# A piece of a weight matrix loaded as two transfers of 64 rows, in an attention and feed-forward kernel with a written-out order

## Chip, cores and metric

The kernel runs on one core of a Trainium2 chip. The core has a matrix engine (TensorE, in the profile PE, with its weight loads as PEld), a vector engine (VectorE, DVE), an engine for activation functions (ScalarE, ACT), a general one (GpSimd, POOL) and a queue engine that here only issues transfers (SyncE, SP). The transfers themselves run on 16 DMA engines, which the profile shows as one share. The metric is the time of the core on the device, in microseconds (us).

## What is computed

Two stages: an attention with 8 batches, 8 heads, 576 positions and 64 values a head, and a feed-forward layer on its 4608 tokens of 512 values.

```python
# attention: a pooled one (every 4 positions averaged) plus a local one (|i - j| < 4)
out_d = sm_attn(q_d, k_d, v_d)                  # softmax attention on 144 pooled positions
out_up = np.repeat(out_d, 4, axis=2)
scores = np.where(mask, scale * q @ k.T, -1e9)  # mask: |i - j| < 4
attn = softmax(scores)
x = (out_up + attn @ v)  -> [4608, 512]
# feed-forward
h = x @ w_in                                    # [512, 1024], in float64 as w_out and g_ln
solu = h * softmax(h)
ln = (solu - mean) / sqrt(var + 1e-6) * g_ln
return (ln @ w_out).astype(np.float32)
```

The weights come as 64-bit floats, the rest as 32-bit floats.

## The kernel before

Per batch, q and k are loaded and transposed, so that the 64 values of a head lie along the partitions; for the first two batches on PE against an identity (`EarlyBatch.pair_steps`, tiles qp and kp, L495), later on DVE. Sums over 4 positions (L380) give the pooled q and k (tiles qd_all and kd). The pooled attention (`Pooled`, tiles sd, pd, po) and the local one in windows of 64 positions (`Local`, L538 to L594, and `PairOfLocals`, tiles sc, pl, plt, xp) add up in a tile x for each batch; v is loaded in three forms (tiles vs, vt and vw).

The feed-forward layer works on 36 tiles of 128 tokens. `xhl` splits x into a high part xh and a low part xl. `ffn_in` multiplies: h takes 24 matmuls a tile (L778), three products (xh with wi_h, xh with wi_l, xl with wi_h) for 4 blocks of rows of w_in and 2 halves of its columns. After softmax and normalizing, the tile goes to DRAM and back in another order (L826, L858), is transposed on DVE (L879), split into uh (ACT, L885) and ul (POOL or DVE, L888), and `ffn_out` multiplies by wo_h and wo_l (L902).

The weights are converted first, in 16 pieces: pieces 0 to 7 are w_in, 8 to 15 w_out. A piece of w_in is 128 rows of 512 columns in 64 bits, 4 KB a row. A step `Weights.load` issues its transfer (L324). Then seven steps convert it (`piece` and `f32`): ACT takes the absolute value of the upper word (L333), DVE makes a 32-bit float in four instructions (L335, L339, L344, L348, tile w), ACT rounds it into wi_h (L371; for w_out with the gain ahead of it, L370), and POOL or DVE takes the rest into wi_l (L373). All eight pieces of w_in are needed for the first tile's h, since each piece gives columns of both halves. The raw words lie in a tile stage (pieces 0, 1, 6 and 7, two at a time) or w64 (the others; the profile calls both loads w and stage).

The rows of w_in are taken in the order in which the attention lays its heads: rows d of head r and of head r + 4 stand below each other. So a piece of w_in is two groups of 64 rows of the matrix, far from each other in DRAM, and its source has the shape 2 x 64 x 1024 words:

```python
by_pair = w_in.rearrange("(a r d) c two -> r a d c two", a=2, d=D)
self.src = [
    by_pair[cc, :, :, n * 512:(n + 1) * 512, :] for cc in range(NCC) for n in range(2)
] + [w_out[fc * P:(fc + 1) * P, :, :] for fc in range(NFC)]
```

The order of all work is written out. The function builds a list `plan` of 1871 steps (each a few instructions on one engine, or a transfer), and a table of numbers, `ORDER`, says in which order they are emitted; every engine then carries out its own instructions in that order. 24 of the steps (`keep_clock`, tile warm) are matmuls on zeros that only keep PE running. A second table, `OTHER`, lists the steps that go to the other of two engines (`engine`): for most DVE in place of POOL or ACT. All transfers are issued on SP, one after another.

Of the kernel before, what the change touches and what calls it, by code (L numbers as in the profile page):

```python
# [125 lines left out]
def pooled_local_attention_then_solu_ffn(  # L126
# [10 lines left out]
    nc = tc.nc  # L137
# [7 lines left out]
    NCC = DM // P  # L145
# [27 lines left out]
    def rows(n):  # L173
        return slice(n * 64, n * 64 + 64)
# [891 lines left out]
```

## Time and profile before

| | |
|---|---|
| three runs, us | 651.26 (median), 649.11 to 652.41 |
| the profiled execution, us | 651.89 |
| its span, first to last instruction, us | 650.1 |
| mean granted clock of PE | 0.952 |
| busy, us: PE, DVE, ACT, POOL | 559.6, 461.2, 309.8, 293.7 |
| DMA: moved, time of the packets as a share of 16 engines | 98.61 MB, 58.7% |

How to read the rows in the parts below: a row of the timeline has its start, its length, engine, line, operation, what is written and from what, and how often; behind it, in brackets, how long the engine had been idle and what ended that. A row of a table of stretches has its bounds, its length, and the busy time of PE, PEld, DVE, ACT and POOL in it, with the number of instructions, then the granted clock of PE (1 is full), the mean busy share of the 16 DMA engines and what they moved in GB/s. A row of waits has who waited, for whom, us in total, how often, and the longest. SPq is the time that SP takes to issue a transfer. A row of DMA issues has the size of one transfer and the median time from issue to landing.

### The profile page before, as it was taken

The numbers are of one execution on the slowest core, as the hardware profiler recorded it, in microseconds if no ns is written. First come the engines' busy times: TensorE is split into PE (matmuls) and PEld (weight loads), VectorE is DVE, ScalarE is ACT, GpSimd is POOL, SyncE is SP. The second block draws the span as 40 slices with busy tenths as digits, with TensorE's granted clock in tenths as the row PEclk, the third lists the DMA queues.
The fourth block names the chain that finished last, engine by engine and source line by source line (L and its number), as shares of the span: only waits on it lengthen the run. The fifth ranks groups of instructions, "written<-read, shape, count | busy, mean of one in ns | idle before, by whom it ended". The sixth has DMA issues, their size and how long they took to land.

```text
span 650.1 us, 16688 instructions
## 1 busy us (share of the span) xinstructions
PE 559.6 (86%) x6728; PEld 435.3 (67%) x6728; DVE 461.2 (71%) x724; ACT 309.8 (48%) x645; POOL 293.7 (45%) x443
## 2 busy tenths in 40 slices
PE   3135434998999999799998999999999999999997
PEld 1134233775677677577776777777777778778885
DVE  2333644897989888688976897899878787756442
ACT  1122324676585556336355365555454636354443
POOL 2002424388776764264654845344535325531211
PEclk9996757698999999999998999999999999999999
DMA  2333344978799688668874867795745345422420
GB/s 73 112 97 97 113 114 123 214 159 207 194 194 215 157 219 189 168 137 232 192 187 146 171 191 187 177 198 134 197 139 170 109 149 160 139 98 98 147 99 32
DMA packets 205854, 99.68 MB, mean 153 GB/s; under 512 B 161872, under 2 KB 192080, under 8 KB 205776
## 3 DMA queue, kind: packets, MB, share of 16 engines
q1 hardware_dynamic: 205776, 98.61, 58.7%
q8 instruction: 53, 0.87, 0.6%
q14 instruction: 25, 0.20, 0.1%
HBM read 65.54 MB, written 27.79 MB: 144 GB/s over the span
## 4 chain that ended last, share of the span: by engine, by line
PE 48%; DMA 18%; SPq 15%; DVE 10%; issue 3%; ACT 3%; POOL 2%; DVEq 0%; POOLq 0%; ACTq 0%
PE h L778 20%; PE o L902 20%; DMA w<-in_moe_w_in_dram 3%; SPq L480 3%; SPq L267 3%; DMA v<-u 3%; DMA stage<-in_moe_w_in_dram 2%; SPq L665 2%; DMA vs<-in_v_dram 2%; DMA u<-e 2%; DMA km<-in_k_dram 2%; SPq L858 2%; SPq L324 2%; PE po L754 2%; PE xp L589 1%
## 5 line engine op out<-in xcount | busy, mean ns | idle before, releaser
L778 PE MATMUL h<-wi_h,xh 128*128 128x512 f32 x288 | 118.1, 410 | 5.0 <-DVE e L793 5.0
L902 PE MATMUL o<-wo_h,uh 128*128 128x512 f32 x288 | 117.1, 407 | 3.6 <-ACT osb L909 2.8
L778 PE MATMUL h<-wi_h,xl 128*128 128x512 f32 x288 | 114.4, 397 | 0.0
L778 PE MATMUL h<-wi_l,xh 128*128 128x512 f32 x288 | 114.4, 397 | 0.0
L902 PE MATMUL o<-wo_l,uh 128*128 128x512 f32 x288 | 114.1, 396 | 0.0
L902 PE MATMUL o<-wo_h,ul 128*128 128x512 f32 x288 | 79.7, 399 | 0.0
L778 PEld LDWEIGHTS h<-wi_h,xh 128*128 128x128 f32 x288 | 54.6, 190 | 20.3 <-issue 5.9
L902 PEld LDWEIGHTS o<-wo_h,uh 128*128 128x128 f32 x288 | 54.0, 188 | 18.8 <-ACT osb L909 3.3
L888 POOL TENSOR_TENSOR ul<-v,uh 128x512 fp32r<-128x512 f32 x37 | 49.1, 1332 | 37.3 <-ACT uh L885 18.7
L902 PEld LDWEIGHTS o<-wo_h,ul 128*128 128x128 f32 x288 | 54.7, 190 | 13.3
L778 PEld LDWEIGHTS h<-wi_h,xl 128*128 128x128 f32 x288 | 54.4, 189 | 13.2
L778 PEld LDWEIGHTS h<-wi_l,xh 128*128 128x128 f32 x288 | 54.7, 190 | 11.9
L885 ACT ACTIVATE uh<-v 128x512 fp32r<-128x512 f32 x70 | 42.9, 624 | 40.7 <-DVE v L879 17.0
L902 PEld LDWEIGHTS o<-wo_l,uh 128*128 128x128 f32 x288 | 54.3, 189 | 11.7
L790 ACT ACTIVATE e<-h,nmx 128x1024 f32<-128x1024 f32 x36 | 40.0, 1112 | 44.4 <-DVE nmx L786 44.1
L495 PE MATMUL qp<-ident,qm 96*64 96x96 f32 x192 | 14.7, 328 | 50.7 <-DMA qm<-in_q_dram 50.5
L786 DVE TENSOR_REDUCE nmx<-h 128x1 f32<-128x1024 f32 x36 | 43.7, 1213 | 19.5 <-PE h L778 19.4
L879 DVE STREAM_TRANSPOSE v<-v 128x512 f32<-128x512 f32 x70 | 46.3, 688 | 13.8 <-DMA v<-u 13.8
L793 DVE SCALAR_TENSOR_TENSOR e<-h,e 128x1024 f32<-128x1024 f32 x36 | 43.6, 1212 | 17.4 <-ACT e L790 17.3
L798 POOL TENSOR_SCALAR nmu<-su 128x1 f32<-128x1 f32 x36 | 8.5, 236 | 94.6 <-DVE e L793 87.3
L335 DVE TENSOR_SCALAR w<-w 128x512 f32<-128x512 f32 x15 | 6.5, 440 | 62.6 <-ACT w L333 62.6
L495 PEld LDWEIGHTS qp<-ident,qm 96*64 96x64 f32 x192 | 13.0, 197 | 53.4 <-DMA qm<-in_q_dram 35.7
(124 smaller groups left out, 1113.0 us busy)
## 6 DMA issues: line engine op xcount, KB each, us to landing
u<-e SPq DMA_DIRECT2D x35, 512.0 KB, 3.0
v<-u SPq DMA_DIRECT2D x140, 128.0 KB, 2.9
qm<-in_q_dram SPq DMA_DIRECT2D x32, 288.0 KB, 12.4
km<-in_k_dram SPq DMA_DIRECT2D x32, 288.0 KB, 4.9
out_dram<-osb SPq DMA_DIRECT2D x36, 256.0 KB, 3.0
vs<-in_v_dram SPq DMA_DIRECT2D x64, 128.0 KB, 3.5
vw<-in_v_dram SPq DMA_DIRECT2D x80, 64.0 KB, 2.7
vw<-in_v_dram SPq DMA_DIRECT2D x40, 128.0 KB, 4.1
```

The source lines that it names most:

```text
L267: nc.sync.dma_start(vw[rows(par ^ wi), wi, :, :], v[b, 4 * par:4 * par + 4, s0:s0 + W, :].rearrange("h s d -> s h d"),)
L324: nc.sync.dma_start(hl, self.src[n])
L480: nc.sync.dma_start(t, src[self.b, pr::4].rearrange("h (p t) d -> p h (t d)", t=self.TT))
L495: nc.tensor.matmul(tp[rows(par), t // HT, at:at + self.TP], self.qk[nm, pr][:, par, t], ident[0:self.TP, 0:self.TP], start=True, stop=True,)
L778: nc.tensor.matmul(hps[:, n, :], src[:, cc, :], wt[:, cc, n * 512:(n + 1) * 512], start=(cc == 0 and src is xh and wt is wi_h), stop=(cc = ...
L786: nc.vector.tensor_reduce(out=nmx, in_=hf, op=ALU.max, axis=AX.X, negate=True)
L790: nc.scalar.activation(e, hf, AF.Exp, bias=nmx, scale=1.0, accum_out=se)
L793: nc.vector.scalar_tensor_tensor(out=e, in0=hf, scalar=1.0, in1=e, op0=ALU.mult, op1=ALU.mult, accum_out=su)
L879: nc.vector.transpose(vg, vg)
L885: nc.scalar.activation(uh, tp, AF.Copy)
L888: (usual if v is None else engine(usual, nc.vector)).tensor_tensor(out=ul, in0=tp, in1=uh.bitcast(F32), op=ALU.subtract)
L902: nc.tensor.matmul(o, src[:, j, :], wt[:, 4 * g + j, :], start=(g == 0 and j == 0 and src is uh and wt is wo_h), stop=(g == 1 and j == 3 a ...
```

## The change

`Weights.load` issues a piece of w_in as two transfers, one for each group of 64 rows; w_out is loaded as before. `ORDER` has the same 1871 steps in another order, and `OTHER` has 76 steps in place of 87.

```diff
 ORDER = """
-14 1 10 141 142 143 144 145 22 146 147 148 24 25 26 27 28 29 30 31 149 150 151 152 153 157 32 33
...
+25 24 141 2 142 143 144 11 14 26 145 146 27 28 147 32 148 149 157 29 30 31 150 151 152 153 33
...
 OTHER = """
-27 66 172 239 339 364 486 586 603 697 726 736 776 801 813 873 888 891 893 895 900 909 934 959
...
+172 239 536 543 553 580 637 659 661 699 719 751 776 811 863 865 881 883 940 965 972 984 1009
...
             hl = hl.bitcast(I32).rearrange("p (c two) -> p c two", two=2)
-            nc.sync.dma_start(hl, self.src[n])
+            if n < 2 * NCC:
+                for a in range(2):
+                    nc.sync.dma_start(hl[rows(a)], self.src[n][a])
+            else:
+                nc.sync.dma_start(hl, self.src[n])
             self.raw[n] = hl
```

(`rows(a)` is partitions 64a to 64a + 63. In the changed file the lines behind this place have numbers that are larger by 4.)

SP, from the start of the program, before (qm and km are the loads of q and k, here of batch 0; the last number of a tile is a buffer's):

```order
L324 DMA stage_141<-in_moe_w_in_dram 128x1x1024
L480 DMA qm_0_154<-in_q_dram 96x2x384
L480 DMA km_0_155<-in_k_dram 96x2x384
L324 DMA stage_141<-in_moe_w_in_dram 128x1x1024
L324 DMA w64_2_197<-in_moe_w_in_dram 128x1x1024
L480 DMA qm_0_154<-in_q_dram 96x2x384
L480 DMA km_0_155<-in_k_dram 96x2x384
L480 DMA qm_0_154<-in_q_dram 96x2x384
L480 DMA km_0_155<-in_k_dram 96x2x384
L324 DMA w64_4_272<-in_moe_w_in_dram 128x1x1024
```

and SP at the same place in the changed kernel:

```order
L484 DMA km_0_133<-in_k_dram 96x2x384
L484 DMA qm_0_132<-in_q_dram 96x2x384
L326 DMA stage_136<-in_moe_w_in_dram 64x1024 x2
L484 DMA qm_0_132<-in_q_dram 96x2x384
L326 DMA stage_136<-in_moe_w_in_dram 64x1024 x2
L326 DMA w64_2_188<-in_moe_w_in_dram 64x1024 x2
L484 DMA km_0_133<-in_k_dram 96x2x384
L484 DMA qm_0_132<-in_q_dram 96x2x384
L484 DMA km_0_133<-in_k_dram 96x2x384
L326 DMA w64_4_237<-in_moe_w_in_dram 64x1024 x2
```

The first loads of q and k stand ahead of the first piece now, each piece is two transfers, and the sequence is otherwise nearly the same. It goes on so: the last transfer of the last piece of w_in is the 46th on SP before and the 50th now.

PE, ahead of the first matmul of the feed-forward layer (tile h_0), before; qp_1_3 and kp_1_3 are transposes for batch 1, xp_0 and plt_0 belong to the local attention of batch 0, sc_1 and sd_1 to the attention of batch 1:

```order
L495 MATMUL qp_1_3_815<-ident_82,qm_1_3_811 64x96 x12
L589 MATMUL xp_0_0_845<-plT_0_0_604,vw_0_0_524 64x58 x16
L495 MATMUL kp_1_3_866<-ident_82,km_1_3_863 64x96 x12
L579 MATMUL plt_0_2_880<-ident_82,pl_2_107 128x128 x4
L589 MATMUL xp_0_1_891<-plT_0_1_813,vw_0_1_830 64x58 x16
L538 MATMUL sc_1_0_908<-kT_1_569,qT_1_568 64x64 x16
L716 MATMUL sd_1_0_927<-kd_1_735,qd_all_119 32x144 x24
L959 LDWEIGHTS filler_101
L959 MATMUL warm_3_952<-filler_101 128x512
```

and now:

```order
L499 MATMUL qp_1_3_825<-ident_82,qm_1_3_822 64x96 x12
L593 MATMUL xp_0_0_841<-plT_0_0_619,vw_0_0_467 64x58 x16
L499 MATMUL kp_1_3_862<-ident_82,km_1_3_859 64x96 x12
L583 MATMUL plt_0_2_875<-ident_82,pl_2_107 128x128 x4
L593 MATMUL xp_0_1_896<-plT_0_1_812,vw_0_1_886 64x58 x16
L542 MATMUL sc_1_0_921<-kT_1_551,qT_1_550 64x64 x16
L963 LDWEIGHTS filler_101
L963 MATMUL warm_12_944<-filler_101 128x512
```

Only a filler has moved ahead of sd_1; the first matmul on h is row 108 of PE's program in both.

DVE, around the two sums x_0 that the first h needs, before (w32_7 is the last piece of w_in, w32_10 a piece of w_out, qd_all and kd_1 the pooled q and k of batch 1):

```order
L344 SCALAR_TENSOR_TENSOR w32_7_751<-stage_141,w32_7_751 128x512
L348 SCALAR_TENSOR_TENSOR w32_7_751<-stage_141,w32_7_751 128x512
L516 TENSOR_TENSOR x_0_753<-x_0_753,xp_0_0_845 128x4x116
L348 SCALAR_TENSOR_TENSOR w32_10_803<-w64_10_801,w32_10_803 128x512
L380 TENSOR_REDUCE qd_all_119<-qT_1_568 128x144
L380 TENSOR_REDUCE kd_1_735<-kT_1_569 128x144
L516 TENSOR_TENSOR x_0_753<-x_0_753,xp_0_1_891 128x4x116
```

and now:

```order
L352 SCALAR_TENSOR_TENSOR w32_7_749<-stage_136,w32_7_749 128x512
L352 SCALAR_TENSOR_TENSOR w32_10_817<-w64_10_814,w32_10_817 128x512
L520 TENSOR_TENSOR x_0_762<-x_0_762,xp_0_0_841 128x4x116
L384 TENSOR_REDUCE qd_all_119<-qT_1_550 128x144
L384 TENSOR_REDUCE kd_1_697<-kT_1_551 128x144
L520 TENSOR_TENSOR x_0_762<-x_0_762,xp_0_1_896 128x4x116
```

One conversion has moved ahead of the first sum; the second sum is row 86 of DVE's program before and row 85 now. Over the whole program `OTHER` moves work between the engines: of the subtractions for ul (L888, then L892) DVE has 35 before and 27 now, POOL 37 and 45; of those for xl (L936, L940) DVE has 15 and 12, POOL 25 and 28.

178 rows, old and new, of tables (ORDER, OTHER) are left out of this document.

## The prediction

> **What bounds the kernel now.** I read the page's share of busy time by slices first, because the average hides stages.
>
> ```profile
> span 650.1 us, 16688 instructions
> PE   3135434998999999799998999999999999999997
> DVE  2333644897989888688976897899878787756442
> DMA  2333344978799688668874867795745345422420
> ```
>
> Each digit is 16.25 us. From the eighth slice on, TensorE (PE) stands at 9 nearly everywhere. In the first seven it stands at 1 to 5, VectorE (DVE) at 2 to 6, and the DMA engines at 2 to 4: nothing is busy. So I cut the span at the first matmul of the feed-forward tiles (L778), and asked for the busy time on both sides.
>
> ```profile
> 126.28 0.50 PE L778 MATMUL h<-wi_h,xh 128*128 128x512 f32 x1
> ...
> 0.00:126.28 126.28, 56.46 (x1001) 42.30 (x1001) 53.21 (x93) 34.97 (x76) 32.27 (x39) 0.80 0.41 116
> 126.28:200.00 73.72, 68.64 (x991) 51.17 (x986) 66.93 (x117) 50.76 (x111) 55.64 (x62) 0.98 0.84 196
> 200.00:650.10 450.10, 434.54 (x4744) 341.88 (x4742) 341.01 (x517) 224.04 (x460) 205.75 (x343) 0.99 0.60 157
> ```
>
> The columns behind the length of a stretch are busy us of PE, PE's weight loads, DVE, ACT, POOL, then the granted clock, the DMA share and GB/s. Behind 126.28 us PE is busy 68.64 + 434.54 = 503.2 of 523.8 us: 20.6 us of idle time are left there, so little can be gained. Ahead of it PE is busy for 56.5 of 126.3 us, and no engine more than that. What is waited for there?
>
> ```profile
> ACT w L333 <- DMA stage<-in_moe_w_in_dram: 36.8, 4, 12.1
> ACT w L333 <- DMA w<-in_moe_w_in_dram: 31.9, 4, 10.0
> PE qp L495 <- DMA qm<-in_q_dram: 50.5, 4, 18.6
> ```
>
> Eight waits of ACT, 68.7 us together, each ended by the landing of one of the eight pieces of w_in; and PE's transposes of q wait 50.5 us for q. The stretches in which all compute engines stand still at once, taken together in one question:
>
> ```profile
> 6.51:14.05 7.54, 0.00 (x0) 0.00 (x0) 0.00 (x0) 0.00 (x0) 0.00 (x0) 1.00 0.13 52
> ...
> 105.40:110.77 5.37, 0.00 (x0) 0.00 (x0) 0.00 (x0) 0.00 (x0) 0.00 (x1) 0.61 0.40 117
> sum 45.06, PE 0.00 PEld 0.00 DVE 0.01 ACT 0.01 POOL 0.00; mean PE 0.00 PEld 0.00 DVE 0.00 ACT 0.00 POOL 0.00
> ```
>
> Eight stretches, 45.06 us. The first row holds the reason: with nothing to do but load, only a share of 0.13 of the DMA engines is busy. It is not the only place:
>
> ```profile
> ## 3 DMA queue, kind: packets, MB, share of 16 engines
> ...
> 8.00:14.00 6.00, 0.00 (x0) 0.00 (x0) 0.00 (x0) 0.00 (x0) 0.00 (x0) 1.00 0.13 51
> ...
> 32.00:36.00 4.00, 0.00 (x0) 0.00 (x0) 0.00 (x0) 0.00 (x0) 0.00 (x0) 1.00 0.13 52
> 86.00:92.00 6.00, 0.00 (x0) 0.00 (x0) 0.00 (x0) 0.65 (x1) 0.00 (x0) 0.50 0.13 51
> ```
>
> 2 of 16 engines are 0.125. In all three stretches a piece of w_in is under way, and the rate is the same 51 GB/s. A piece is "one transfer of two groups", two groups of 64 rows, and **it runs on two engines**. The other transfers have to pass these two engines too, so the SyncE queue (SP) comes to stand behind them:
>
> ```profile
> 4.18 7.95 SPq L324 DMA_DIRECT2D w<-in_moe_w_in_dram  x1
> 12.18 9.55 SPq L480 DMA_DIRECT2D qm<-in_q_dram  x1
> ...
> 96.05 0.54 SPq L324 DMA_DIRECT2D stage<-in_moe_w_in_dram  x1
> ...
> stage<-in_moe_w_in_dram SPq DMA_DIRECT2D x4, 512.0 KB
> w<-in_moe_w_in_dram SPq DMA_DIRECT2D x4, 512.0 KB
> ```
>
> An issue that costs 0.54 us when nothing is in its way takes 7.95 and 9.55 us there. Eight pieces of 512 KB (524 KB in thousands) at 51 GB/s are 8 x 10.3 = 82 us of these two engines: most of the 110 us before the last piece has landed.
>
> **The change part by part.** (1) *Each piece as two transfers of 64 rows.* Whether a transfer of 64 plain rows uses more than two engines isn't shown for w_in, but for other tiles it is:
>
> ```profile
> vw<-in_v_dram SPq DMA_DIRECT2D x40, 128.0 KB, 4.1
> v<-u SPq DMA_DIRECT2D x140, 128.0 KB, 2.9
> w<-in_moe_w_out_dram SPq DMA_DIRECT2D x8, 512.0 KB, 5.6
> ```
>
> The first are 64 rows, the last 128 rows of 4 KB, as long as those of w_in. One engine moves 51 / 2 = 25.5 GB/s. At that, 131 KB would take 5.1 us on one engine; they land in 4.1 and 2.9 us (medians, beside other traffic). A piece of w_out with the same bytes lands in 5.6 us, where two engines would need 10.3. So the number of rows in the outer group counts, not the bytes, and I take it that a half of w_in spreads as w_out does: between 2 us (all 16 engines: 524 / 408 = 1.3 us and the way) and 5.6 us in place of 10.3 and more.
>
> The Trainium skill has this as a rule: in "DMA: Bandwidth & Descriptors", section "Why a DMA increments its semaphore by 16 and not by 1", the number of engines is the largest number up to 16 that divides the slowest dimension (not 1) of both sides. By it, before is 2 and the halves are 16, and the trace's 0.13 agrees with the 2; the 16 is shown by no run yet. The same page, section "Rules for kernel authors", says against the change that two transfers to disjoint halves of the partitions only serialize and one of 128 partitions should be used; its sum would be the rival of no gain below.
>
> (2) *Eight more issues on SP.* Up to the last piece there are 46 transfers in SP's row before and 50 after. At 0.54 us these are 27 us, less than the loading takes in any case, so they are hidden; uncovered, 8 x 0.54 = 4.3 us.
>
> (3) *What is late next.* The first matmul on h needs all eight pieces converted, and the sums of batch 0. The rows of order above show PE and DVE with nearly the same work ahead of it as before. So I ask when it can start, engine by engine.
>
> ```profile
> 123.37:126.28 2.91, 2.85 (x93) 1.64 (x85) 2.65 (x5) 2.51 (x6) 1.78 (x2) 0.95 1.15 183
> 0.00:14.71 14.71, 4.07 (x8) 0.89 (x8) 2.11 (x7) 1.94 (x2) 3.86 (x14) 1.00 0.23 76
> ...
> 92.00:102.00 10.00, 8.99 (x177) 8.51 (x185) 9.39 (x16) 6.48 (x13) 7.64 (x8) 0.78 0.73 187
> ...
> 26.00:28.00 2.00, 0.00 (x0) 0.00 (x0) 1.16 (x3) 0.66 (x1) 0.00 (x0) 1.00 0.80 245
> ...
> 14.05 0.66 ACT L333 ACTIVATE w<-stage 128x512 f32<-128x512 f32 x1 [12.05 <-DMA stage<-in_moe_w_in_dram]
> 14.74 0.43 DVE L335 TENSOR_SCALAR w<-w 128x512 f32<-128x512 f32 x1 [11.60 <-ACT w L333]
> 15.21 0.43 DVE L339 TENSOR_SCALAR w<-w 128x512 int32<-128x512 int32 x1
> 15.67 0.69 DVE L344 SCALAR_TENSOR_TENSOR w<-stage,w 128x512 int32<-128x512 int32 x1
> 16.39 0.69 DVE L348 SCALAR_TENSOR_TENSOR w<-stage,w 128x512 int32<-128x512 int32 x1
> 17.12 0.63 ACT L371 ACTIVATE wi_h<-w 128x512 fp32r<-128x512 f32 x1 [2.41 <-DVE w L348]
> 17.90 1.26 POOL L373 TENSOR_TENSOR wi_l<-w,wi_h 128x512 fp32r<-128x512 f32 x1 [13.23 <-ACT wi_h L371]
> ...
> L959 PE MATMUL warm<-filler 128*128 128x512 bf16 x28 | 12.8, 553 | 2.6 <-POOL filler L203 2.3
> ```
>
> DVE: 53.21 us by the first h, less the 2.65 behind the last sum that h needs and the 2.11 of memsets at the start: 48.45 us. Where its data is there, DVE is busy 91% (66.93 of 73.72 us, above) to 94% (the third row): 48.45 / 0.91 = 53.2 us. It starts when the first transfers are in (the first 1.1 MB at 245 GB/s are 4.5 us; with 2.5 us until bytes flow and ACT's 0.7 us, 7.7 us), and from its last sum to h are 2.9 us. Sum: **63.8 us**.
>
> DMA: ahead of the end of the last piece 9792 KB are issued (w_in 4096, 14 loads of q and k of 288, the rest v): 10.03 MB. At 187 GB/s (third row) 53.6 us, at 245 GB/s 40.9; with 2.5 us ahead and 4.8 us for converting the last piece (ACT 0.66 and 0.63, DVE 2.24, POOL 1.26; the rows at 14.05 to 17.90), 48 to 61 us. PE has 56.5 us, at a clock of 0.80, with 12.8 us of fillers among it: less when it is warm. ACT (35.0) and POOL (32.3) are below.
>
> So DVE sets it, with the DMA close behind. Two limits as near as this don't overlap fully; I add 3 us, an estimate, and take **67 us** for the first h, 126.28 - 67 = 59.3 us sooner. Bounds: not later than 126.28 - 45.06 = 81.2 us (only the joint stalls go, every chain stays as it is), not sooner than 7.7 + 48.45 + 2.9 = 59.0 us (DVE without a gap).
>
> (4) *The order searched anew, and other engines chosen.* Behind the first h the work is the same. By the rows of order, 8 of the subtractions for ul go from DVE to POOL:
>
> ```profile
> L888 POOL TENSOR_TENSOR ul<-v,uh 128x512 fp32r<-128x512 f32 x37 | 49.1, 1332 | 37.3 <-ACT uh L885 18.7 <-DMA v<-u 12.1 <-DMA u<-e 4.1
> L888 DVE TENSOR_TENSOR ul<-v,uh 128x512 fp32r<-128x512 f32 x33 | 26.9, 822 | 10.9 <-ACT uh L885 8.7 <-POOL s L842 2.1
> ```
>
> Each is 0.51 us longer there, 4.1 us if all were on the path; DVE gets 6.6 us back. POOL has room (293.7 us busy). I take nothing for it. From -7 us (a third of the 20.6 us of idle time closed) to +3 us (most of the 4.1 shows).
>
> **Sum.** The profiled execution took 651.89 us, its span 650.1 and 1.8 around it; it lies 0.6 us above the median of the runs, 651.26. 651.26 - 59.3 = **592.0 us**.
>
> **The rivals.** *A chain, not DVE, sets the start* (for it: each piece goes ACT, DVE four times, ACT, POOL, and PE's transposes wait for ACT's copies; against: DVE at 94% between 92 and 102 us): only the stalls go, 651.26 - 45.06 = 606.2 us. *More than that*: DVE without gaps and the idle time behind h partly closed, 651.26 - 67.3 - 7 = 577 us or less. *The change doesn't do what it says*: both halves go through the same two engines, a piece takes 10.3 us as before; 8 issues are hidden, 651 us. For it speaks only that no row shows a half; against it w_out's 5.6 us. *The other side*: a transfer of a single group runs on a single engine, as one of two groups runs on two, and both halves on the same one. Then a piece takes 20.6 us at 25.5 GB/s, eight of them 164 us and not 82, and the end moves to 651.26 + 82 = 733 us; this decides as soon as both halves together get under 51 GB/s. Against it are the 64-row transfers of 128 KB in 4.1 us.
>
> **How the numbers follow.** Forecast (577 to 600 us) 0.62; chain (600 to 612) 0.24; more than forecast (under 577) 0.05; a gain between 7 and 40 us 0.02; no gain 0.04; slower 0.03. The range of 577 to 609 us reaches from DVE without gaps to the chain with 3 us on top; it holds nearly all of the first two cases. A measurement of this kernel can tell about 0.5% (3 us) from no change: faster 0.93, same 0.04, slower 0.03.
>
> **What would show it.** The DMA share in the first 60 us should be 0.6 or more and never stand at 0.13 with the engines idle; ACT's waits for w_in should fall from 68.7 us to under 15; SP's long issues should vanish; the first L778 matmul (L782 in the changed file) should start at 59 to 81 us, and the time behind it should be 517 to 527 us. Wrong would be the forecast if the share of 0.13 stays, or if PE loses more than 25 us behind its first h.

## The result, and the profile after

The changed kernel takes 602.6 us (median of 4 runs, 599.1 to 605.7) against 651.4 before (649.1 to 652.4): a ratio of 0.925, interval 0.919 to 0.932. 48.8 us are gone; 59.3 were forecast. All medians below are of fast runs; one run of a later kernel (w_in in four parts) was in a slower state of the chip and is left out.

The shares by slices of the changed kernel, from its page, with 14.9 us a digit:

```profile
span 597.3 us, 16706 instructions
...
PE   4878969899799999999998989999899999999996
...
DVE  4899968887795988988878688788758577555541
...
DMA  9999978869697775878659875488552562434321
```

The slow start is gone: PE reaches 8 in the second slice, and the DMA engines, at 2 to 4 before, stand at 9 from the first slice. The table of stretches, cut at the first matmul on h again (L782 now), once with the rest split as before, and for DVE the 36 us ahead of that matmul:

```profile
0.00:66.02 66.02, 48.36 (x1001) 35.88 (x1001) 53.00 (x92) 35.74 (x78) 35.33 (x40) 0.82 0.95 211
66.02:139.74 73.72, 65.20 (x964) 48.76 (x960) 60.75 (x106) 44.68 (x91) 52.45 (x60) 0.93 0.83 181
...
66.02:597.30 531.28, 506.51 (x5733) 396.22 (x5728) 395.40 (x624) 272.45 (x565) 271.85 (x417) 0.98 0.64 161
...
30.00:66.02 36.02, 28.64 (x735) 21.35 (x733) 34.61 (x60) 24.27 (x60) 26.11 (x22) 0.86 0.94 209
```

The first h starts at 66.02 us and not at 126.28: 60.3 us sooner. Ahead of it DVE has as much work as before (53.0 us; 53.2 before) in half the time, and is busy for 34.61 of the last 36.02 us, with the DMA share at 0.94 beside it. Behind the first h the stretch has become longer: 531.3 us, where it was 523.8. In the first 73.7 us of it PE is busy for 65.20 us, where it was 68.64. The waits for w_in ahead of the first h:

```profile
ACT L337 <- DMA stage<-in_moe_w_in_dram: 8.3, 1, 8.3
...
ACT w L337 <- DMA w<-in_moe_w_in_dram: 0.3, 1, 0.3
```

8.6 us are left of 68.7, nearly all of it the wait for the first piece. SP's queue at the place of the long issues, and the sizes and landings of the halves:

```profile
4.67 1.24 SPq L326 DMA_DIRECT2D w<-in_moe_w_in_dram  x2
5.95 0.58 SPq L484 DMA_DIRECT2D km<-in_k_dram  x1
7.01 0.32 SPq L484 DMA_DIRECT2D qm<-in_q_dram  x1
...
stage<-in_moe_w_in_dram SPq DMA_DIRECT2D x8, 256.0 KB, 5.9
w<-in_moe_w_in_dram SPq DMA_DIRECT2D x8, 256.0 KB, 6.2
```

No issue there takes 8 us any more. The halves land in 5.9 and 6.2 us (medians, beside other traffic).

### The profile page after: what moved, and what is told of

It reads as the page before. It is cut to its first block, busy times and chain, and to the rows that moved or that the text cites. A ratio compares the mean times of both kernels' runs of the same rounds, so it can differ in the third digit from the quotient of the medians.

```text
span 597.3 us, 16706 instructions
## 1 busy us (share of the span) xinstructions
PE 554.9 (93%) x6728; PEld 432.1 (72%) x6728; DVE 448.4 (75%) x714; ACT 308.2 (52%) x641; POOL 307.2 (51%) x457
## 4 chain that ended last, share of the span: by engine, by line
PE 68%; DMA 10%; SPq 7%; DVE 5%; POOL 4%; issue 4%; ACT 1%; POOLq 0%; DVEq 0%; ACTq 0%
PE o L906 27%; PE h L782 26%; DMA km<-in_k_dram 3%; PE po L758 2%; PE sc L623 2%; PE sd L720 2%; PE xp L681 2%; DMA v<-u 1%; SPq L267 1%; PE sc L542 1%; PE plt L583 1%; DMA w<-in_moe_w_in_dram 1%; DMA stage<-in_moe_w_in_dram 1%; PE xp L593 1%; DMA qm<-in_q_dram 1%
## 5 line engine op out<-in xcount | busy, mean ns | idle before, releaser
L782 PE MATMUL h<-wi_h,xh 128*128 128x512 f32 x288 | 118.3, 411 | 2.5 <-DVE e L797 2.5
L782 PE MATMUL h<-wi_h,xl 128*128 128x512 f32 x288 | 115.1, 399 | 0.0
L782 PE MATMUL h<-wi_l,xh 128*128 128x512 f32 x288 | 115.0, 399 | 0.0
L892 POOL TENSOR_TENSOR ul<-v,uh 128x512 fp32r<-128x512 f32 x45 | 58.2, 1299 | 30.5 <-ACT uh L889 29.9
L782 PEld LDWEIGHTS h<-wi_h,xh 128*128 128x128 f32 x288 | 54.9, 191 | 17.0 <-issue 3.2
L782 PEld LDWEIGHTS h<-wi_h,xl 128*128 128x128 f32 x288 | 54.8, 190 | 13.5 <-DVE xl L940 0.2
L782 PEld LDWEIGHTS h<-wi_l,xh 128*128 128x128 f32 x288 | 54.9, 191 | 12.0
L940 POOL TENSOR_TENSOR xl<-x,xh 128x512 fp32r<-128x512 f32 (+1 forms) x28 | 32.9, 1181 | 23.0 <-ACT xh L937 22.6
L820 ACT ACTIVATE e<-e,nmu 128x1024 f32<-128x1024 f32 x26 | 29.8, 1148 | 25.0 <-POOL nmu L802 25.0
L913 ACT ACTIVATE osb<-o,s 128x512 f32<-128x512 f32 x36 | 24.5, 680 | 32.2 <-PE o L906 15.7
```

Source lines behind the costliest of these rows:

```text
L782: nc.tensor.matmul(hps[:, n, :], src[:, cc, :], wt[:, cc, n * 512:(n + 1) * 512], start=(cc == 0 and src is xh and wt is wi_h), stop=(cc = ...
L820: nc.scalar.activation(e, e, AF.Identity, bias=nmu, scale=1.0)
L892: (usual if v is None else engine(usual, nc.vector)).tensor_tensor(out=ul, in0=tp, in1=uh.bitcast(F32), op=ALU.subtract)
L913: nc.scalar.activation(osb, o, AF.Copy, scale=s)
L940: engine(nc.gpsimd, nc.vector).tensor_tensor(out=l, in0=src, in1=h.bitcast(F32), op=ALU.subtract)
```

## The experiments

Two things were to be settled: whether it is the number of DMA engines that brought the gain, and where the 7.5 us behind the first h come from. All of them in one table; "first h" and "behind it" are from one profiled execution each, the medians and ratios from 4 runs a kernel (10 for 62 + 2, 3 for the four parts) beside runs of the kernel before on the same chip (650.8 to 651.6 us).

| kernel | w_in as | ORDER, OTHER | first h, us | behind it, us | median, us | ratio to before (95%) |
|---|---|---|---|---|---|---|
| before | 2 groups | old, old | 126.28 | 523.8 | 651.3 | |
| changed | 64 + 64 | new, new | 66.02 | 531.3 | 602.6 | 0.925 (0.919 to 0.932) |
| changed, once more | 64 + 64 | new, new | 67.89 | 536.4 | 603.5 | 0.926 (0.920 to 0.931) |
| split alone | 64 + 64 | old, old | 68.02 | 524.2 | **594.6** | 0.914 (0.910 to 0.918) |
| tables alone | 2 groups | new, new | 125.11 | 531.7 | 659.1 | 1.013 (1.009 to 1.017) |
| cut by columns | 2 groups, twice | new, new | 125.03 | 533.1 | 660.2 | 1.015 (1.011 to 1.019) |
| one plain group | 128 | new, new | 68.59 | 527.9 | 598.3 | 0.921 (0.915 to 0.927) |
| four parts | 4 x 32 | new, new | 64.84 | 535.6 | 602.2 | 0.926 (0.920 to 0.932) |
| odd parts | 62 + 2 + 62 + 2 | old, old | 125.42 | 522.7 | 653.5 | 1.003 (1.000 to 1.007) |
| mixed | 64 + 64 | new, old | 65.29 | 548.4 | 620.3 | 0.951 (0.947 to 0.955) |
| mixed | 64 + 64 | old, new | 68.25 | 536.2 | 605.8 | 0.931 (0.927 to 0.936) |
| one load of v earlier | 64 + 64 | new', new | 69.43 | 539.0 | 603.1 | 0.928 (0.923 to 0.934) |
| w_out issued on ACT | 64 + 64 | new, new | 66.15 | 546.2 | 613.6 | 0.942 (0.936 to 0.948) |
| w_out issued on ACT | 64 + 64 | old, old | 67.52 | 532.2 | 601.7 | 0.925 (0.919 to 0.931) |

**The split alone.** The diff's load, with ORDER and OTHER of before.

> The split alone, with ORDER and OTHER of before. Theory 'engines' (a w_in transfer with two groups runs on 2 of 16 DMA engines, one of 64 rows on all): the first matmul on h starts at 64 to 72 us as in the changed kernel (66.02) and not at 126.28; the time is 592 to 612 us. Within it: if the 7.5 us that the changed kernel lost behind the first h (531.3 against 523.8 us) come from its new ORDER and OTHER, 592 to 597 us; if they come from the DMA work that now falls into a shorter time, 600 to 612 us. Theory 'order' (the new order brought the gain): about 650 us.

594.6 us: better than the changed kernel by 8.0 us, and 2.6 us from the forecast of 592.0. Its two stretches, from its table:

```profile
0.00:68.02 68.02, 51.21 (x1000) 37.56 (x1000) 54.70 (x94) 35.56 (x77) 33.28 (x39) 0.80 0.94 216
68.02:592.20 524.18, 503.35 (x5735) 392.86 (x5728) 406.58 (x632) 274.93 (x570) 261.56 (x404) 0.99 0.64 162
```

The first h comes 58.3 us sooner, the rest is as long as before (524.2 and 523.8 us). So the load brings the whole gain, and the denser start shows no cost behind it.

**The tables alone.**

```diff
-            if n < 2 * NCC:
-                for a in range(2):
-                    nc.sync.dma_start(hl[rows(a)], self.src[n][a])
-            else:
-                nc.sync.dma_start(hl, self.src[n])
+            nc.sync.dma_start(hl, self.src[n])
```

> The new ORDER and OTHER with the load of before. Theory 'engines': stretches with a DMA share of 0.13 are back, first h at 120 to 130 us, 645 to 665 us. Theory 'order': 600 to 606 us, as the changed kernel.

659.1 us, slower than before by 8 us. With the split alone this makes a table of four: the load takes off 56.3 us with the old tables (650.8 to 594.6) and 56.5 with the new (659.1 to 602.6); the tables add 8.3 us without the split and 8.0 with it. The two don't depend on each other.

**Two transfers of two groups each**, cut by columns:

```diff
-                for a in range(2):
-                    nc.sync.dma_start(hl[rows(a)], self.src[n][a])
+                for c in range(2):
+                    cs = slice(256 * c, 256 * c + 256)
+                    nc.sync.dma_start(hl[:, cs, :], self.src[n][:, :, cs, :])
```

> The changed kernel, but a piece is cut by columns: two transfers, each of two groups of 64 rows with half a row (2 KB). Same number of transfers and bytes, still two groups. Theory 'engines': two engines again, share 0.13, first h at 118 to 130 us, 645 to 665 us. Rival 'two in flight' (it is the number of transfers under way that counts, not their shape): 600 to 610 us.

660.2 us: as the tables alone. Twice as many transfers of the same shape bring nothing. In its stretches of 2 us the share is back; in these three all compute engines stand still:

```profile
10.00:12.00 2.00, 0.00 (x0) 0.00 (x0) 0.00 (x0) 0.00 (x0) 0.00 (x0) 1.00 0.13 51
12.00:14.00 2.00, 0.00 (x0) 0.00 (x0) 0.00 (x0) 0.00 (x0) 0.00 (x0) 1.00 0.13 51
...
34.00:36.00 2.00, 0.00 (x0) 0.00 (x0) 0.00 (x0) 0.00 (x0) 0.00 (x0) 1.00 0.13 50
```

**One plain group of 128 rows, one transfer**, of neighbouring rows of w_in, which are not the rows that the product needs, so the output is not the layer's:

```diff
-                for a in range(2):
-                    nc.sync.dma_start(hl[rows(a)], self.src[n][a])
+                cc, half = divmod(n, 2)
+                nc.sync.dma_start(hl, w_in[cc * P:(cc + 1) * P, half * 512:(half + 1) * 512, :])
```

> The changed kernel, but a piece is 128 neighbouring rows of w_in, in one transfer (another set of rows than the matrix product wants: the rows of w_in are mixed up in the output). Same bytes, one group, 8 transfers fewer. Theory 'engines': all 16 engines, first h at 63 to 67 us, 596 to 604 us; against the changed kernel, 0 to 4.3 us less for 8 issues of 0.54 us. Rival 'two in flight': 640 to 660 us.

598.3 us: the gain without a second transfer. The first h, at 68.59 us, is a little later than was expected. The time is 4.3 us below the changed kernel, at the upper end of what 8 issues were to cost, but its runs reach from 596.4 to 604.7 and overlap with those of the changed kernel, so the price of the issues isn't measured by it.

**Four transfers of 32 rows:**

```diff
-                for a in range(2):
-                    nc.sync.dma_start(hl[rows(a)], self.src[n][a])
+                for g in range(4):
+                    a, d = divmod(g, 2)
+                    nc.sync.dma_start(
+                        hl[32 * g:32 * g + 32], self.src[n][a][32 * d:32 * d + 32]
+                    )
```

> The changed kernel, a piece as four transfers of 32 rows: 16 issues more, 32 rows still spread over 16 engines by the theory 'engines'. If an issue on SP costs only where SP is late: 600 to 608 us, first h within 2 us of 66.02. If each issue counts in full (0.54 us): 16 x 0.54 = 8.6 us more, 611 us. If 32 rows use fewer engines: later still.

602.2 us with the first h at 64.84: 16 issues more are hidden (8.6 us if they counted in full), and 32 rows spread as 64 do (share 0.94 ahead of the first h, where it was 0.95).

**62 rows and 2 rows**, with the old tables:

```diff
-                    nc.sync.dma_start(hl[rows(a)], self.src[n][a])
+                    for lo, hi in ((0, 62), (62, 64)):
+                        nc.sync.dma_start(hl[64 * a + lo:64 * a + hi], self.src[n][a][lo:hi])
```

> The split alone with the order of before (594.6 us), but each group of 64 rows is loaded as 62 rows and 2 rows: 32 transfers for w_in. Theory 'divisor' (a transfer uses the largest number of engines up to 16 that divides its rows: 62 gives 2): the share of 0.13 is back although every transfer has one plain group, first h at 115 to 130 us, 640 to 665 us. Rival 'spread' (any group of many rows spreads over all engines): first h at 66 to 75 us, 592 to 610 us.

Every transfer has one plain group now, and the gain is gone: 653.5 us beside 594.6 for 64 rows. From its table of stretches:

```profile
8.00:14.00 6.00, 0.00 (x0) 0.00 (x0) 0.00 (x0) 0.00 (x0) 0.00 (x0) 0.66 0.13 51
...
0.00:125.42 125.42, 55.53 (x1000) 41.68 (x1000) 53.60 (x93) 35.28 (x76) 32.09 (x39) 0.65 0.43 114
```

The share of 0.13 and the 51 GB/s are back. The 32 transfers by themselves are not the reason: four parts of 32 rows are as many. So it isn't the group itself that counts but the number of rows that are dealt out: 62 go to two engines, 32, 64 and 128 to many more. (What a transfer of 2 rows does can't be told apart here.) The rule of the Trainium skill weighed in the prediction ("DMA: Bandwidth & Descriptors", "Why a DMA increments its semaphore by 16 and not by 1") says this for 62: the largest number up to 16 that divides it is 2. The runs agree with it for 2 groups and 62 rows (share 0.13) and for 32, 64 and 128 rows (shares of 0.94, 0.95 and 0.91 ahead of the first h, other loads among them). They don't tell the largest divisor from the largest power of two, which is 2 for 62 as well. The Trainium skill's advice on the same page, section "Rules for kernel authors", to use one transfer of 128 partitions rather than two halves does not hold for this case: the one transfer has a slowest (outermost) dimension of 2, and the kernel takes 650.8 us with it and 594.6 with the halves. With a plain group of 128 rows, one transfer does as well as two (598.3 us, with the new tables).

**Which of the tables costs the 8 us?** The split with one table new and one old:

```diff
 ORDER = (new)
-OTHER = (new: 172 239 536 543 ...)
+OTHER = (old: 27 66 172 239 339 ...)
```

> The split with the new ORDER and the OTHER of before. The split alone took 594.6 us, the changed kernel 602.6: 8 us lie in ORDER or OTHER. Theory 'order on SP' (the new ORDER puts loads of v behind loads of batch 2 and w_out, and PE waits for them behind the first h): 600 to 606 us. Rival 'engines chosen' (8 subtractions for ul on POOL, 0.5 us longer each, stand on the path): 592 to 597 us.

> The split with the ORDER of before and the new OTHER. Theory 'order on SP': 592 to 598 us, about as the split alone. Rival 'engines chosen': 600 to 606 us.

Neither theory holds for both runs. 620.3 us with the new ORDER and the old OTHER, 605.8 the other way round: the second lies in the range of "engines chosen" (600 to 606), but the first is far outside both ranges. Each mixture is worse than either pair that was made together (602.6 and 594.6), so the 8 us can't be put down to one table.

**One load of v earlier.** Behind the first h, PE of the changed kernel waits for loads of v; the kernel before has 1.3 us. From the waits of both (of the changed kernel between 66.02 and 200 us), and the changed kernel's timeline:

```profile
PE xp L589 <- DMA vw<-in_v_dram: 1.3, 2, 1.0
...
PE xp L593 <- DMA vw<-in_v_dram: 7.3, 6, 4.2
...
81.07 0.43 PE L593 MATMUL xp<-plT,vw 64*64 64x58 f32 x2 [4.25 <-DMA vw<-in_v_dram]
...
75.20 5.98 SPq L267 DMA_DIRECT2D vw<-in_v_dram  x8
```

SP issues them from 75.2 us on, behind loads of batch 2. In this kernel the step that loads windows 6 and 7 of batch 0 stands ahead of those:

```diff
 ORDER = """
-... 125 431 218 424 611 ... 419 273 274 116 613 ...
+... 125 431 116 218 424 611 ... 419 273 274 613 ...
```

> The changed kernel with one step moved in ORDER: the load of v for window pair 3 of batch 0 (step 116, four transfers on SP) stands behind step 431, ahead of three loads of k, one of q and one piece of w_out. PE waited 4.25 and 0.96 us for it at 81 us. Theory 'order on SP': that wait goes, 596 to 601 us (2 to 6 us less than the changed kernel). Rival (what SP issues later instead is waited for, or the wait is hidden): 601 to 605 us.

603.1 us, no change. From its timeline and its waits (this profiled execution took 610.1 us, the longest of its four):

```profile
63.77 6.93 SPq L279 DMA_DIRECT2D vw<-in_v_dram  x8
...
91.54 0.36 PE L605 MATMUL xp<-plT,vw 64*64 64x56 f32 x2 [0.88 <-DMA vw<-in_v_dram]
...
PE xp L605 <- DMA vw<-in_v_dram: 6.2, 6, 2.7
```

The row at 63.77 us holds four transfers that stood there before and then the four that were moved, from 67.24 us on, 8 us sooner. The wait at 81 us is gone, but the loads that were passed come later (the next load of k at 70.74 us and not at 66.64), and PE waits for other loads of v: 6.2 us in place of 7.3.

**w_out issued on ACT**, to take eight issues off SP; once with the new tables and once with the old:

```diff
             else:
-                nc.sync.dma_start(hl, self.src[n])
+                nc.scalar.dma_start(hl, self.src[n])
```

> The changed kernel (602.6 us) with the eight loads of w_out issued on ACT and not on SP. Theory 'SP late': behind the first h, SP issues loads of v too late because it is issuing without a pause; with eight issues fewer (0.4 to 2.9 us each there) PE's waits for vw shrink, 595 to 600 us. Rival 'bytes' (the loads land late because the DMA engines are at a share of 0.8 to 1.0): within 2 us of 602.6. Rival 'ACT held' (ACT has to wait for a buffer before it may issue): 603 to 615 us.

> The split alone with the order of before (594.6 us), w_out issued on ACT. If SP is late there too: 589 to 593 us; if not: 593 to 597; if ACT is held: above 597.

Both are slower, by 11.0 us (10.1 beside the repeat below) and 7.2 us. ACT's waits in the changed kernel, and its waits and timeline in the first of these two, show why:

```profile
ACT w L337 <- DMA w<-in_moe_w_out_dram: 1.9, 1, 1.9
...
ACT w L337 <- DMA w<-in_moe_w_out_dram: 23.3, 5, 5.8
...
71.20 0.33 ACTq L328 DMA_DIRECT2D w<-in_moe_w_out_dram  x1
76.03 0.66 ACT L337 ACTIVATE w<-w 128x512 f32<-128x512 f32 x1 [5.38 <-DMA w<-in_moe_w_out_dram]
```

SP runs ahead of the work; ACT doesn't. On ACT a load is issued in ACT's own order, here 4.8 us ahead of the instruction that needs it, and ACT then stands for the landing: 23.3 us in five waits, where it was 1.9 us in one with the loads on SP. The time is in the range of "ACT held", but that rival had ACT waiting for a buffer, not for the landing. PE's wait for loads of v at L593 does fall, from 7.3 to 3.7 us; what that alone is worth stays open, since the new wait covers it.

**The changed kernel once more**, word for word:

> The changed kernel once more, word for word, beside the others on one chip: 599 to 606 us, first h at 64 to 70 us.

603.5 us. A single execution of it differs from the next in the stretch behind the first h by 5 us (531.3 and 536.4), so differences of a few us between two single profiles of this table aren't read.

## Why the prediction was right, and where it was off

*Two engines for a piece (1)*: right, and the ground of everything: share 0.13 with two groups, cut by columns or not, and 0.9 and more with 64 rows. That a half would spread "as w_out does" held, though the halves landed in 5.9 and 6.2 us, a little above the 2 to 5.6 us given for them. (The 1.3 us in that lower bound is the time of a whole piece on 16 engines; a half would take 0.6.) It cost little: ACT waits 0.3 us for w_in behind the first piece. The rival in which a single group runs on a single engine, and the one in which the halves share the two engines, are refuted by the changed kernel itself.

*Eight more issues (2)*: hidden, as costed; sixteen more are hidden too.

*What is late next (3)*: right. The first h was put at 67 us (59.0 to 81.2): 66.02 and 67.89 with the new tables, 68.02 with the old. DVE set it, as far as the profile shows (96% busy from 30 us on), with the DMA engines at 0.94 close behind; no run takes the two apart. The forecast rate of 187 GB/s was a little low (211).

*The order searched anew (4)*: this term was mis-sized. "Behind the first h the work is the same", "I take nothing for it", with at most 3 us of loss. It measured 7.5 and 12.6 us in two executions, and 8.0 us by medians, the same without the split (8.3). That is the larger part of the 10.6 us between forecast and result; the other 2.6 us are what the split alone lies above the forecast. Two of the prediction's own signs are about this term. The time behind the first h was to be 517 to 527 us, and is 531.3 and 536.4. PE was to lose no more than 25 us there: it stands still for 24.8 us in the first execution and 29.8 in the repeat, where it was 20.6.

The stretches show where. From the kernel before, the changed kernel and its repeat:

```profile
200.00:260.26 60.26, 58.34 (x760) 45.63 (x766) 52.49 (x83) 34.38 (x63) 39.53 (x61) 1.00 0.82 187
...
139.74:200.00 60.26, 56.26 (x629) 43.84 (x628) 46.51 (x75) 31.76 (x69) 35.52 (x51) 0.94 0.85 201
...
67.89:604.30 536.41, 506.61 (x5735) 396.31 (x5728) 398.01 (x626) 273.69 (x567) 273.73 (x418) 0.98 0.63 160
...
PE o L906 <- POOL ul L892: 3.0, 1, 3.0
...
155.72 1.04 POOL L561 TENSOR_TENSOR pl<-pl,mxl 128x512 f32<-128x512 f32 x1 [4.78 <-DVE mxl L559]
...
159.05 1.26 POOL L892 TENSOR_TENSOR ul<-v,uh 128x512 fp32r<-128x512 f32 x1
```

With the stretches of 73.72 us shown above, PE is busy for 121.5 of the first 134 us behind h, where it was 127.0: it stands still for 5.5 us more, and behind that for 1.4 us less. It is busy for 3.3 us more behind h with the same matmuls (506.5 and 503.2 us), at a granted clock of 0.93 and 0.94 in the two stretches where it was 0.98 and 1.00.

PE's longer waits there are those for loads of v (7.3 us, where it was 1.3) and, once, for a subtraction for ul on POOL (3.0 us), which on POOL comes behind a step of the attention that had to wait 4.78 us for DVE (the last two rows). So a subtraction on POOL, a term set aside because POOL had room, does hold PE up, but by its place in the order and not by the 0.51 us that it takes longer: such a wait of 2.3 to 3.8 us stands in eight of the nine profiles with the new ORDER, also in the one with the old OTHER (3.7 us), and in none of the five with the old ORDER. How much of the 8 us each of these waits makes up stays open: no run takes the wait for ul away, and moving one late load only passed the other on.

The prediction gave 0.62 to 577 to 600 us and 0.24 to 600 to 612, the chain; the measured time lies in the second. That rival, "a chain, not DVE", would have given 606.2 us, near the measured time, but for the wrong reason: it had the first h at 81 us, and it was at 66.

The best version run is the split with the old tables, 594.6 us, 8 us faster than the changed kernel.

## What to carry to other kernels

When every engine is idle and the DMA share is a small and constant fraction, multiply it by the number of DMA engines: 0.13 x 16 = 2 says that a transfer is dealt out over two, and the shape of its slowest (outermost) dimension tells why. Cut such a transfer so that each part has a number of rows with a large divisor up to 16 (32, 64 and 128 did here, 62 did not), and don't count transfers or bytes. When a change of code comes with a new order, run the code with the old order too: here one gave 56 us, and the other took 8 back. And an engine with idle time on average can still be waited for: look at single waits before a term is put at nothing.

## What the runs showed of the hardware

62 rows are loaded at the pace of two groups (51 GB/s, share 0.13), and 2 x 62 + 2 x 2 rows cost 59 us more than 2 x 64 in this kernel (653.5 and 594.6 us). The transfers on two engines held up other loads too: behind the first three of them, the issue of a load of q took 9.55 us on SP; with 64 rows, issues of q and k at that place took 0.3 to 0.6 us, also in the split alone, where the order is the same.
